# Token-mixing weights in two rings, first copies on two engines, and an order made with the time between successive operations

## The chip, the cores and the metric

The kernel runs on one core of a Trainium2 chip. A core has five engines, each with an instruction stream of its own that it works off in order: TensorE (PE in the profile; PEld is its loading of weights, which overlaps the matmuls), VectorE (DVE), ScalarE (ACT), GpSimd (POOL) and SyncE (SP), which here only issues DMAs. An instruction waits at the head of its stream until what it needs is there, and all that stand behind it wait too. The metric is the device time of one execution in microseconds (us); the median of the runs is what counts.

## The reference: what is computed

```
scores = q @ k.T / sqrt(64);  rel = i - j                      # 4 batches, 8 heads, 576 tokens, 64 wide
scores = where(0 <= rel < 128, scores - slope_h * |rel|, -1e9) # a causal window with a linear bias
x = softmax(scores) @ v                                        # -> (4, 576, 512)
xt = x.transpose(0, 2, 1)
u = x + (relu(xt @ w_tok1) @ w_tok2).transpose(0, 2, 1)        # token mixing, 576 -> 256 -> 576
u = u + relu(u @ w_ch1) @ w_ch2                                # channel layer, 512 -> 1536 -> 512
y = u + relu(layernorm(u) * g @ b_ch1) @ b_ch2                 # channel layer, 512 -> 2048 -> 512
```

## The kernel before

The 2304 tokens are 18 tiles of 128 rows. The attention goes tile by tile. For tile i TensorE makes the scores of its two halves of heads (bank `ps_s`, L625); VectorE merges the two key tiles by a predicated copy (L660) and adds the bias while it takes the row's extreme (L666); ScalarE takes the exponentials and their sums (L675, eight of 128 columns a tile); TensorE transposes them (L682, into `ps_t`, one bank); ScalarE copies the transposed half to `pf` (L384); GpSimd cuts it by the two triangles (L692); TensorE multiplies by `v` (L637, into the one bank `ps_v`, in one piece with the scores of a later tile); ScalarE copies the sum to `ut`, TensorE transposes it back (L704), VectorE divides (L400, `u`).

A finished tile goes into the token mixing. Every such product is made as three matmuls of a rounded part and a remainder (`xh`, `xl`; `wt1h`, `wt1l`): L469 to L471 for the first matrix, L764 to L766 for the second, whose weights lie in `fewh` and `fewl`. ScalarE makes the rounded parts, GpSimd most remainders of weights and tiles, in two halves each. The channel layers follow from about 140 us, by seven products instead of eight (L1125 to L1127) and second products (L1238 to L1240, L1275), each with its own conversions.

The weights lie in DRAM as 64-bit floats, and `load_f64` (L410) converts a piece on the chip: one DMA brings the bytes with the exponents ("heads", tile `rh`), one the bytes with the fractions (`rw`). ScalarE reads `rh` (L445, to `e`), VectorE makes sign and exponent `s` (L448, L450), the fraction `m` (L452) and the value `y` (L460); then ScalarE rounds `y` and GpSimd takes the remainder. There is one buffer `rh` and there are two `rw`, for all weights: the next piece's heads are sent for when ScalarE has read the last. The first token matrix is five pieces of 256 columns, the second four of 288; the ring `w` of six tiles (pool `wa`) stays empty until the channel weights come, from the 12th half tile on.

What stands where on each engine is decided when the program is built. The planner (class `Plan`, L121) takes operations with a cost for each engine that can do them, plays them through engine by engine, and takes at each engine the available one with the earliest due time (`ranks`, L207, `order`, L223). `LAT` (L136) is what it adds between the end of an operation and the start of one that needs it; `dve`, `act`, `pool_tt` and `pe` (L313 to L334) give costs by columns. Remainders and sums may go to VectorE or GpSimd, whichever it finds ready sooner, with 1200 ns to VectorE's disadvantage (`SPARE`). `TOK_RATE` lets three steps of token mixing follow each half tile.

Of the kernel before, what the change touches and what calls it, by code (L numbers as in the profile page):

```python
# [24 lines left out]
P = 128  # L25
# [7 lines left out]
RING = 4  # L33
CT = 4
# [86 lines left out]
class Plan:  # L121
# [14 lines left out]
    LAT = {"PE": 400, "DVE": 260, "ACT": 290, "POOL": 180, "DMA": 4000, "CTL": 0}  # L136
# [192 lines left out]
def pe(n):  # L329
    return 2.6 + n / 2.4  # L330


def pe2(n):
    return 13 + n / 2.4  # L334


def block_kernel(tc, qT, kT, v, wt1, wt2, wa1, wa2, wb1, wb2, g, bias, out):
# [72 lines left out]
    def load_f64(src, k, n, dst=None, get=None):  # L410
# [5 lines left out]
        rh = buf("raw", [P, DM, 4], I16, "rh", 1)  # L416
# [10 lines left out]
        def head(dt):  # L427
            return rh.t[:, :n, 3].bitcast(dt) if dt != I16 else rh.t[:, :n, 3]

        def load_half(x, first):  # L430
            def emit():
                out, in_ = rows(x.t[:, :n].bitcast(U8), first)
                nc.sync.dma_start(out=out, in_=in_)

            op({"DMA": max(P * n * 8 / 360, 500)}, emit, writes=[x])

        load_half(rh, at)
        load_half(rw, at + 3)

        def half(x):  # L440
# [5 lines left out]
            out=e.t[:, :n], in_=head(BF16), func=AF.Copy, scale=2.0 ** -116), [rh], [e])  # L446

        op({"DVE": 1.3 * dve(n // 2, True)}, lambda: nc.vector.tensor_scalar(  # L448
            half(s), half(e), 3, EXP16, ALU.logical_shift_left, ALU.bitwise_and), [e], [s])
        op({"DVE": 1.3 * dve(n // 2)}, lambda: nc.vector.scalar_tensor_tensor(  # L450
            out=half(s), in0=half(e), scalar=SIGN16, in1=half(s), op0=ALU.bitwise_and, op1=ALU.bitwise_or), [e], [s])
        op({"DVE": 1.3 * dve(n, True)}, lambda: nc.vector.tensor_scalar(  # L452
# [7 lines left out]
        op({"DVE": 1.3 * dve(n)}, lambda: nc.vector.scalar_tensor_tensor(  # L460
            out=get(), in0=m.t[:, :n], scalar=2.0 ** 32, in1=s.t[:, :n], op0=ALU.add, op1=ALU.mult), [m, s], [dst])
# [120 lines left out]
    def load_wt2(j):  # L582
        kt, c = divmod(j, 2)
        w = S // 2
# [22 lines left out]
    def packed(i, i2):  # L607
# [21 lines left out]
        if i2 is not None:  # L629
            tiles2 = keys_of(i2)[0]  # L630
            na = len(tiles2)
            for c in range(2):
# [7 lines left out]
                parts.append((na * 440, values, [(pf_t[i2, c], a) for a in range(na)] + [vs[kt] for kt in tiles2],  # L640
# [11 lines left out]
    def softmax(i, c):  # L652
# [5 lines left out]
        if na == 2:  # L658
            b = slice((1 - own) * P, (2 - own) * P)
            op({"DVE": 690}, lambda: nc.vector.copy_predicated(  # L660
# [4 lines left out]
        for m in range(4):  # L665
            op({"DVE": 358}, lambda m=m: nc.vector.tensor_tensor_reduce(  # L666
# [7 lines left out]
        for m in range(4):  # L674
            op({"ACT": 580}, lambda m=m: nc.scalar.activation(  # L675
# [8 lines left out]
        op({"PE": 400}, transposes, [pr, ident], [pt])  # L684

        pf = pf_t[i, c] = buf("atb", [P, 2, 4, P], F32, "pf", PF_BUFS)
        if na == 1:
            copy((pf, 0), lambda: pf.t[:, 0], pt, lambda: pt.t, 4 * P, ("ACT",), True)
        else:
            copy((pf, 1), lambda: pf.t[:, 1], pt, lambda: pt.t, 4 * P, ("ACT",), True)  # L690
            for a in range(2):
                op({"POOL": 630}, lambda a=a: nc.gpsimd.affine_select(  # L692
# [3 lines left out]
    def normalize(i):  # L696
# [3 lines left out]
        copy(ut, lambda: ut.t, pv, lambda: pv.t, DM, ("ACT",), True)  # L700
# [5 lines left out]
        op({"PE": 400}, transposes, [ut, ident], [pv])  # L706
# [44 lines left out]
    def tok2(i):  # L751
        parts = batches_of(i)
        o = buf("pst", [P, DM], F32, "tok", 2)
        for m, (b, r0, n, s0) in enumerate(parts):
# [3 lines left out]
            for kt in range(2):  # L758
                hh, hl = h1_t[b, kt]
                pieces = ["zero"] + sorted({kt * 2 + first // (S // 2), kt * 2 + (end - 1) // (S // 2)})  # L760
# [15 lines left out]
    def attention():  # L776
# [37 lines left out]
        for i in range(-1, NTILE + 1):  # L814
# [15 lines left out]
            for c in range(2):  # L830
# [29 lines left out]
    def turned(layer, places):  # L860
# [6 lines left out]
        if layer == 1:  # L867
            x = buf("mlp", [P, 4, P], F32, "st", ST_BUFS)
            for j, (i, k) in enumerate(places):
                op({"ACT": 330}, lambda i=i, j=j, g=get[j]: nc.scalar.activation(  # L870
# [9 lines left out]
        op({"PE": 430}, emit, [*xs, ident], [b])  # L880
# [367 lines left out]
    def second_fast(s, w2, hid):  # L1248
# [17 lines left out]
        def product(group, x, h, w, start, stop):  # L1266
# [11 lines left out]
            op({"PE": 6 * pe2(HW)}, emit, [hh, hl, wh, wl], [o])  # L1278
# [202 lines left out]
```

## Time and profile before

| | us |
|---|---|
| median of 3 runs (lowest, highest) | 834.79 (834.41, 836.09) |
| profiled execution, whole | 835.71 |
| profiled execution, span of its instructions | 834.0 |
| PE busy | 820.6 (98%) |
| PEld, DVE busy | 691.7 (83%), 658.4 (79%) |
| POOL, ACT busy | 466.4 (56%), 430.8 (52%) |
| TensorE's granted clock | 1.00 in every slice but the last |

The profiled execution is 1.7 us longer than its span, and 0.9 us over the median. Busy times are shares of a span with several stages: attention and token mixing to about 140 us, the channel layers after that. A matmul's end is modelled, so a PE that is shown as busy may still start its next matmul late; the wait of a weight load (PEld) then shows it.

### The profile page before, as it was taken

Reading aid. Unit: us, or ns where it says so; the run is one execution under the profiler, and the core shown is the slowest. Engines: PE = TensorE matmul, PEld = TensorE weight load, DVE = VectorE, ACT = ScalarE, POOL = GpSimd, SP = SyncE. Lnnn points to the kernel's source line nnn. Section 1 sums busy time; section 2 is a strip of 40 time slices with the busy share of each in tenths; the row PEclk is TensorE's granted clock in tenths of the full one; section 3 lists DMA queues with packets and bytes.
Section 4 is the critical chain, followed back from the end, with each engine's and each line's share of the span. In section 5 each row is a group of like instructions: output and inputs, shape, how many; then the busy total and the mean of one; then the engine's idle time right before and its main releaser. Section 6 shows DMA issues by size and latency. Waiting matters only on the chain.

```text
span 834.0 us, 14315 instructions
## 1 busy us (share of the span) xinstructions
PE 820.6 (98%) x4732; PEld 691.7 (83%) x4732; DVE 658.4 (79%) x1372; ACT 430.8 (52%) x1015; POOL 466.4 (56%) x708
## 2 busy tenths in 40 slices
PE   8998999999999999999999999999999999999998
PEld 6777788888888898888888888888889889999996
DVE  5786878978898989978889868989666767777785
ACT  6887777633344535234368333447456634444440
POOL 2685366755454667543338666857533656666650
PEclk9999999999999999999999999999999999999999
DMA  8679657443678799977861544888977663443202
GB/s 301 194 215 275 227 173 224 134 158 111 232 252 283 272 335 334 348 266 266 269 238 55 186 158 137 296 306 299 356 250 243 219 226 136 131 141 122 103 26 101
DMA packets 79898, 179.20 MB, mean 215 GB/s; under 512 B 9040, under 2 KB 9168, under 8 KB 79824
## 3 DMA queue, kind: packets, MB, share of 16 engines
q1 hardware_dynamic: 79344, 176.98, 63.3%
q0 software_dynamic: 480, 1.31, 0.6%
q8 instruction: 37, 0.61, 0.3%
q14 instruction: 37, 0.30, 0.1%
HBM read 138.15 MB, written 38.80 MB: 212 GB/s over the span
## 4 chain that ended last, share of the span: by engine, by line
PE 90%; DVE 3%; DMA 3%; ACT 1%; POOL 1%; issue 1%; SPq 0%; ACTq 0%; DVEq 0%; POOLq 0%
PE tok L1238 11%; PE tok L1240 11%; PE tok L1239 10%; PE b L1125 10%; PE b L1126 10%; PE b L1127 10%; PE tok L1275 5%; PE p L1275 4%; PE ps_v L637 3%; PE ps_s L625 2%; PE p L878 2%; PE b L471 2%; PE b L470 2%; PE b L469 2%; PE tok L766 1%; PE tok L764 1%
## 5 line engine op out<-in xcount | busy, mean ns | idle before, releaser
L1243 DVE TENSOR_TENSOR u<-tok,u 128x512 f32<-128x512 f32 x196 | 133.8, 685 | 47.8 <-PE tok L1240 46.1
L1238 PE MATMUL tok<-w2h,hh 128*128 128x512 f32 x392 | 154.2, 393 | 0.2 <-DVE u L1243 0.2
L1240 PE MATMUL tok<-w2h,hl 128*128 128x512 f32 x392 | 153.0, 390 | 0.2 <-DVE hl L958 0.2
L1239 PE MATMUL tok<-w2l,hh 128*128 128x512 f32 x392 | 152.9, 390 | 0.0
L1125 PE MATMUL b<-xh,w1h 128*128 128x512 f32 x384 | 150.4, 392 | 0.0
L1126 PE MATMUL b<-xl,w1h 128*128 128x512 f32 x384 | 149.8, 390 | 0.0
L1127 PE MATMUL b<-xh,w1l 128*128 128x512 f32 x384 | 149.5, 389 | 0.0
L402 POOL TENSOR_TENSOR w1l<-w,w1h 128x256 fp32r<-128x256 f32 (+1 forms) x110 | 77.4, 725 | 103.5 <-ACT w1h L384 99.0
L956 ACT ACTIVATE hh<-b 128x512 fp32r<-128x512 f32 (+1 forms) x112 | 58.7, 542 | 147.1 <-PE b L1127 104.1
L958 DVE SCALAR_TENSOR_TENSOR hl<-b,hh 128x512 fp32r<-128x512 f32 (+1 forms) x112 | 67.4, 617 | 26.3 <-ACT hh L956 25.7
L1240 PEld LDWEIGHTS tok<-w2h,hl 128*128 128x128 f32 x392 | 73.6, 188 | 16.4 <-DVE hl L958 0.8
L1238 PEld LDWEIGHTS tok<-w2h,hh 128*128 128x128 f32 x392 | 73.7, 188 | 15.5 <-DVE u L1243 1.3
L402 POOL TENSOR_TENSOR w1l<-st,w1h 128x256 fp32r<-128x256 f32 x70 | 55.3, 811 | 55.5 <-ACT w1h L384 49.7
L1239 PEld LDWEIGHTS tok<-w2l,hh 128*128 128x128 f32 x392 | 73.7, 188 | 14.3
L1127 PEld LDWEIGHTS b<-xh,w1l 128*128 128x128 f32 x384 | 72.1, 188 | 15.4
L1125 PEld LDWEIGHTS b<-xh,w1h 128*128 128x128 f32 x384 | 72.3, 188 | 13.9 <-DVE b L400 0.2
L1126 PEld LDWEIGHTS b<-xl,w1h 128*128 128x128 f32 x384 | 72.2, 188 | 13.5
L445 ACT ACTIVATE e<-rh 128x512 bf16<-128x512 bf16 (+2 forms) x65 | 41.5, 639 | 62.1 <-DMA rh<-wb 35.6
L675 ACT ACTIVATE pr<-t,mn 128x128 f32<-128x128 f32 x144 | 55.9, 392 | 13.7 <-DVE mn L666 13.7
L692 POOL TENSOR_SCALAR_AFFINE_SELECT pf<-pf 128x512 f32<-128x512 f32 x64 | 42.5, 663 | 30.1 <-ACT pf L384 27.9
L400 DVE TENSOR_TENSOR b<-b,p 128x512 f32<-128x512 f32 x56 | 38.9, 694 | 19.8 <-PE b L1127 18.7
L402 POOL TENSOR_TENSOR st<-w 128x128 f32<-128x128 f32 x68 | 37.3, 573 | 24.1 <-PE tok L1240 5.5
(188 smaller groups left out, 1909.7 us busy)
## 6 DMA issues: line engine op xcount, KB each, us to landing
w<-d SPq DMA_DIRECT2D x86, 256.0 KB, 4.1
rw<-wb SPq DMA_DIRECT2D x32, 512.0 KB, 5.3
rh<-wb SPq DMA_DIRECT2D x32, 512.0 KB, 5.3
rw<-wa SPq DMA_DIRECT2D x24, 512.0 KB, 4.5
rh<-wa SPq DMA_DIRECT2D x24, 512.0 KB, 4.4
d<-y SPq DMA_DIRECT2D x30, 256.0 KB, 5.0
keys<-kT SPq DMA_DIRECT2D x18, 256.0 KB, 4.3
q<-qT SPq DMA_DIRECT2D x18, 256.0 KB, 4.5
```

Source lines behind the costliest of these rows:

```text
L402: ENGINE[e].tensor_tensor(get()[:, c], ga()[:, c], gb()[:, c], alu)
L675: op({"ACT": 580}, lambda m=m: nc.scalar.activation(out=pr.t[:, m], in_=t.t[:, m], func=AF.Exp, bias=mn.t[:, m:m + 1], scale=-1.0, accum_o ...
L956: op({"ACT": act(n, True)}, lambda: nc.scalar.activation(out=hh.t[:, c], in_=go(), func=AF.Relu), [o], [(hh, key)])
L958: mark[0] = op({"DVE": dve(n)}, lambda: nc.vector.scalar_tensor_tensor(out=hl.t[:, c], in0=go(), scalar=0.0, in1=hh.t[:, c].bitcast(F32), ...
L1125: nc.tensor.matmul(g.t, wh.t[:, w], xh.t, start=start and k == 0, stop=False, skip_group_check=True)
L1126: nc.tensor.matmul(g.t, wh.t[:, w], xl.t, start=False, stop=False, skip_group_check=True)
L1127: nc.tensor.matmul(g.t, wl.t[:, w], xh.t, start=False, stop=stop and k == 1, skip_group_check=True)
L1238: nc.tensor.matmul(o.t, hh.t[:, c:c + P], wh.t, start=j == 0, stop=False)
L1239: nc.tensor.matmul(o.t, hh.t[:, c:c + P], wl.t, start=False, stop=False)
L1240: nc.tensor.matmul(o.t, hl.t[:, c:c + P], wh.t, start=False, stop=j == 1)
L1243: op({"DVE": dve(DM)}, lambda o=o, i=i: nc.vector.tensor_tensor(u[i].t, o.t, u[i].t, ALU.add), [o], [u[i]])
L1275: nc.tensor.matmul(o.t[:, p], x()[:, c], y(), start=start and p == 0 and k == 0, stop=stop and p == 1 and k == 2, skip_group_check=True)
```

## The change

It does four things. (1) `load_f64_split` sends the heads of every second piece of the two token matrices to a tile of the ring `w` instead of `rh`, and reads them there. (2) The second token matrix is loaded in 3 pieces of 192 columns for each half instead of 2 of 288, six in all, and the second token product names those pieces. (3) In the first three tiles (`FIRST_TILES`) the copies `pf` and `ut` may go to VectorE too. (4) The planner's costs are set to other numbers: VectorE's, ScalarE's and GpSimd's fixed part is smaller, a 128x512 matmul costs 10 ns more, the exponential 385 in place of 580, the extreme 211 in place of 358, and the latencies are larger. With them the planner makes another order for the whole program. TensorE's instructions are the same in number and shape (4732 matmuls).

```diff
+WT2_PARTS, FIRST_TILES = 3, 3
-    LAT = {"PE": 400, "DVE": 260, "ACT": 290, "POOL": 180, "DMA": 4000, "CTL": 0}
+    LAT = {"PE": 400, "DVE": 340, "ACT": 400, "POOL": 230, "DMA": 4000, "CTL": 0}
...
 def dve(n, fast=False):
-    return 150 + n / (1.92 if fast else 0.97)
+    return 70 + n / (1.92 if fast else 0.97)
 def act(n, psum=False, pointers=0):
-    return 170 + (0.82 if psum else 0.9) * n + 93 * pointers
+    return 60 + (0.82 if psum else 0.9) * n + 93 * pointers
 def pool_tt(n):
-    return 150 + 2.4 * n
+    return 130 + 2.25 * n
 def pe(n):
-    return 2.6 + n / 2.4
+    return 13 + n / 2.4
...
-    def load_f64(src, k, n, dst=None, get=None):
+    def load_f64(src, k, n, dst=None, get=None, heads=None):
-        rh = buf("raw", [P, DM, 4], I16, "rh", 1)
+        if heads is None:
+            rh = buf("raw", [P, DM, 4], I16, "rh", 1)
+
+            def raw_heads():
+                return rh.t[:, :n]
+        else:
+            rh, raw_heads = heads
...
-        load_half(rh, at)
-        load_half(rw, at + 3)
+        load_half(rh, raw_heads, at)
+        load_half(rw, lambda: rw.t[:, :n], at + 3)
...
+    turn_heads = [0]
+
     def load_f64_split(hi, ghi, lo, glo, src, k, n):
-        split(hi, ghi, lo, glo, *load_f64(src, k, n), n, ("ACT",), ("POOL",))
+        heads = None
+        turn_heads[0] ^= 1
+        if not turn_heads[0]:
+            x = buf("wa", [P, DM], F32, "w", W_BUFS)
+            heads = x, lambda: x.t.bitcast(I16).rearrange("p (n t) -> p n t", t=4)[:, :n]
+        split(hi, ghi, lo, glo, *load_f64(src, k, n, heads=heads), n, ("ACT",), ("POOL",))
...
     def load_wt2(j):
-        kt, c = divmod(j, 2)
-        w = S // 2
+        kt, c = divmod(j, WT2_PARTS)
+        w = S // WT2_PARTS
...
-            op({"DVE": 358}, lambda m=m: nc.vector.tensor_tensor_reduce(
+            op({"DVE": 211}, lambda m=m: nc.vector.tensor_tensor_reduce(
...
-            op({"ACT": 580}, lambda m=m: nc.scalar.activation(
+            op({"ACT": 385}, lambda m=m: nc.scalar.activation(
...
+        on = ("ACT", "DVE") if i < FIRST_TILES else ("ACT",)
         pf = pf_t[i, c] = buf("atb", [P, 2, 4, P], F32, "pf", PF_BUFS)
         if na == 1:
-            copy((pf, 0), lambda: pf.t[:, 0], pt, lambda: pt.t, 4 * P, ("ACT",), True)
+            copy((pf, 0), lambda: pf.t[:, 0], pt, lambda: pt.t, 4 * P, on, True)
...
-        copy(ut, lambda: ut.t, pv, lambda: pv.t, DM, ("ACT",), True)
+        copy(ut, lambda: ut.t, pv, lambda: pv.t, DM, ("ACT", "DVE") if i < FIRST_TILES else ("ACT",), True)
...
-                elif r == 0 and 5 <= m < 9:
+                elif r == 0 and 5 <= m < 5 + 2 * WT2_PARTS:
                     load_wt2(m - 5)
...
-    arrays["wt2"] = rows(w2.reshape(2, P, 2, S // 2).transpose(0, 2, 1, 3), S // 2)
+    arrays["wt2"] = rows(w2.reshape(2, P, WT2_PARTS, S // WT2_PARTS).transpose(0, 2, 1, 3), S // WT2_PARTS)
```

SyncE's stream of DMAs, after the loads of the first tiles; before, where the numbers behind the names only tell buffers apart:

```order
L376 DMA v_189<-v 128x512
L433 DMA rh_199<-wt1 128x2048
L796 DMA bias_sb_131<-bias 128x2048
L561 DMA keys_108<-kT 128x512
L376 DMA q_228<-qT 128x512
L433 DMA rw_238<-wt1 128x2048
L433 DMA rw_245<-wt1 128x2048
```

The same place now:

```order
L373 DMA v_198<-v 128x512
L805 DMA bias_sb_131<-bias 128x2048
L568 DMA keys_108<-kT 128x512
L373 DMA q_226<-qT 128x512
L433 DMA rh_239<-wt1 128x2048
L433 DMA rw_248<-wt1 128x2048
L433 DMA w_253<-wt1 128x2048
L433 DMA rw_261<-wt1 128x2048
L433 DMA w_270<-wt1 128x2048
L433 DMA w_280<-wt2 128x1536
```

The first heads have moved behind the bias table, the keys and the queries of the fifth tile; five more loads of weights follow them at once, three of these into `w`. ScalarE's stream still has the read of the first heads (L445) ahead of the first copy to `ut`, as before.

TensorE's stream after the first values of the second tile; before (`ps_t` is the transpose of exponentials, `ut` the copied sum):

```order
L682 MATMUL ps_t_412<-ident_101,pr_340 128x128 x4
L704 MATMUL ps_v_271<-ident_101,ut_420 128x128 x4
L469 MATMUL tok_444<-xh_395,wt1h0_384 128x512
L470 MATMUL tok_444<-xl_422,wt1h0_384 128x512
L471 MATMUL tok_444<-xh_395,wt1l0_405 128x512
L469 MATMUL tok_452<-xh_395,wt1h0_384 128x512
```

The same place now:

```order
L689 MATMUL ps_t_437<-ident_101,pr_350 128x128 x4
L476 MATMUL tok_447<-xh_370,wt1h0_374 128x512
L477 MATMUL tok_447<-xl_394,wt1h0_374 128x512
L478 MATMUL tok_447<-xh_370,wt1l0_410 128x512
L476 MATMUL tok_459<-xh_370,wt1h0_374 128x512
L477 MATMUL tok_459<-xl_394,wt1h0_374 128x512
L478 MATMUL tok_459<-xh_370,wt1l0_410 128x512
L712 MATMUL ps_v_275<-ident_101,ut_453 128x128 x4
```

The transpose that needs `ut` has gone from ahead of six token matmuls to behind them; from the second to the ninth tile it now has three or six of them in front, where before it had none or three.

VectorE's stream where a tile's scores come in; before:

```order
L709 RECIPROCAL rc_489<-rc_489 128x8
L400 TENSOR_TENSOR u_324<-ps_v_271,rc_400 128x512
L448 TENSOR_SCALAR s_558<-e_479 128x128
L450 SCALAR_TENSOR_TENSOR s_558<-e_479,s_558 128x128
L460 SCALAR_TENSOR_TENSOR y_568<-m_473,s_558 128x256
L452 TENSOR_SCALAR m_577<-rw_362 128x256
L660 COPY_PREDICATED ps_s_585<-after_111,ps_s_585 128x4x128
L660 COPY_PREDICATED ps_s_594<-after_111,ps_s_594 128x4x128
```

The sixth tile now:

```order
L397 TENSOR_TENSOR u_338<-ps_v_275,rc_372 128x512
L717 RECIPROCAL rc_613<-rc_613 128x8
L448 TENSOR_SCALAR s_627<-e_619 128x128
L667 COPY_PREDICATED ps_s_608<-after_111,ps_s_608 128x4x128
L450 SCALAR_TENSOR_TENSOR s_627<-e_619,s_627 128x128
L667 COPY_PREDICATED ps_s_622<-after_111,ps_s_622 128x4x128
```

The step on a piece's heads that needs ScalarE's `e` now stands directly ahead of the tile's predicated copies, or between them, in the fourth to the seventh tile. Over the whole program VectorE has 46 instructions more: 8 for the two added pieces, 2 copies `pf`, and 36 remainders and sums that were on GpSimd, most of 512 columns, nearly all in the channel layers.

## Rows read from the trace of the kernel before

**Rows 1.** Busy time by stretch: PE, PEld, DVE, ACT, POOL; clock, DMA share, GB/s.
```profile
0.00:20.00 20.00, 15.86 (x124) 12.87 (x124) 10.66 (x62) 14.26 (x57) 5.29 (x20) 1.00 0.86 303
20.00:68.00 48.00, 45.38 (x442) 35.34 (x439) 37.69 (x166) 40.59 (x149) 36.42 (x65) 1.00 0.74 208
68.00:76.00 8.00, 5.84 (x59) 4.27 (x58) 4.59 (x23) 4.27 (x15) 2.27 (x6) 1.00 0.92 314
...
100.00:834.00 734.00, 729.53 (x3913) 620.49 (x3912) 587.25 (x1048) 353.16 (x729) 411.45 (x600) 1.00 0.62 211
```

**Rows 2.** Waits of PE in the whole span: us in total, times, longest.
```profile
PE ps_v L704 <- ACT ut L384: 1.5, 3, 0.7
...
PE tok L470 <- POOL xl L402: 0.8, 2, 0.4
PE tok L766 <- POOL fewl L402: 0.6, 1, 0.6
PE tok L1275 <- DVE u L1243: 0.4, 1, 0.4
PE tok L764 <- ACT fewh L384: 0.3, 1, 0.3
PE tok L1238 <- DVE u L1243: 0.2, 1, 0.2
PE tok L1240 <- DVE hl L958: 0.2, 1, 0.2
```

**Rows 3.** Waits of PE's weight loads from 5 to 100 us.
```profile
PEld ps_v L704 <- ACT ut L384: 2.9, 5, 0.9
...
PEld tok L470 <- POOL xl L402: 1.8, 3, 0.7
```

**Rows 4.** ACT in order of time: start, us, instruction, idle time before it and releaser.
```profile
72.45 0.46 ACT L445 ACTIVATE e<-rh 128x288 bf16<-128x288 bf16 x1 [3.73 <-DMA rh<-wt]
72.82 0.58 ACT L384 ACTIVATE pf<-ps_t 128x512 f32<-128x512 f32 x1
```

**Rows 5.** DMA issues from 8.5 to 11.9 us: count, size, us to landing.
```profile
bias_sb<-bias SPq DMA_DIRECT2D x1, 512.0 KB, 6.0
rh<-wt SPq DMA_DIRECT2D x1, 256.0 KB, 5.4
keys<-kT SPq DMA_DIRECT2D x1, 256.0 KB, 5.9
q<-qT SPq DMA_DIRECT2D x1, 256.0 KB, 5.9
```

**Rows 6.** SyncE in order of time: when two of those were issued.
```profile
8.84 0.33 SPq L433 DMA_DIRECT2D rh<-wt  x1
...
10.94 0.33 SPq L376 DMA_DIRECT2D q<-qT  x1
```

**Rows 7.** ACT in order of time, at the first piece's heads.
```profile
14.46 0.43 ACT L445 ACTIVATE e<-rh 128x256 bf16<-128x256 bf16 x1
14.79 0.58 ACT L384 ACTIVATE ut<-ps_v 128x512 f32<-128x512 f32 x1
```

**Rows 8.** PE in order of time: a transpose, the scores of tiles 4 and 9.
```profile
15.43 0.66 PE L704 MATMUL ps_v<-ident,ut 128*128 128x128 f32 x4 [0.16 <-ACT ut L384]
...
18.32 2.00 PE L625 MATMUL ps_s<-keys,q 64*128 64x256 f32 x16
...
55.43 2.00 PE L625 MATMUL ps_s<-keys,q 64*128 64x256 f32 x16
```

**Rows 9.** Groups by line and shape, ACT up to 80 us: busy us, mean ns.
```profile
L675 ACT ACTIVATE pr<-t,mn 128x128 f32<-128x128 f32 x88 | 34.1, 392 | 8.1 <-DVE mn L666 8.1
...
L384 ACT ACTIVATE xh<-u 128x512 fp32r<-128x512 f32 x7 | 4.3, 621 | 0.0
```

**Rows 10.** Groups by line and shape, DVE in the whole span.
```profile
L1243 DVE TENSOR_TENSOR u<-tok,u 128x512 f32<-128x512 f32 x196 | 133.8, 685 | 47.8 <-PE tok L1240 46.1
...
L400 DVE TENSOR_TENSOR w1l<-w,w1h 128x512 fp32r<-128x512 f32 x10 | 7.6, 760 | 1.1 <-ACT w1h L384 0.8
```

More of the change, by code (lines that the diff above doesn't have):

```diff
@@ L425, in rows, with load_half @@
             return x.rearrange("p n t -> p (n t)"), flat[first:first + P * n * 8].rearrange("(p b) -> p b", p=P)
-        def head(dt):
-            return rh.t[:, :n, 3].bitcast(dt) if dt != I16 else rh.t[:, :n, 3]
-        def load_half(x, first):
+        def load_half(x, get, first):
             def emit():
-                out, in_ = rows(x.t[:, :n].bitcast(U8), first)
+                out, in_ = rows(get().bitcast(U8), first)
                 nc.sync.dma_start(out=out, in_=in_)
             op({"DMA": max(P * n * 8 / 360, 500)}, emit, writes=[x])
-        load_half(rh, at)
-        load_half(rw, at + 3)
+        load_half(rh, raw_heads, at)
+        load_half(rw, lambda: rw.t[:, :n], at + 3)
         def half(x):
@@ L638, in values @@
                                                  pf.t[:, a, 2 * p + j], start=(a == 0), stop=(a == na - 1))
-                parts.append((na * 440, values, [(pf_t[i2, c], a) for a in range(na)] + [vs[kt] for kt in tiles2],
+                parts.append((na * 480, values, [(pf_t[i2, c], a) for a in range(na)] + [vs[kt] for kt in tiles2],
                               [(pv, c)]))
@@ L682, in transposes @@
                 nc.tensor.transpose(pt.t[:, m], pr.t[:, m], ident.t)
-        op({"PE": 400}, transposes, [pr, ident], [pt])
+        op({"PE": 436}, transposes, [pr, ident], [pt])
+        on = ("ACT", "DVE") if i < FIRST_TILES else ("ACT",)
         pf = pf_t[i, c] = buf("atb", [P, 2, 4, P], F32, "pf", PF_BUFS)
         if na == 1:
-            copy((pf, 0), lambda: pf.t[:, 0], pt, lambda: pt.t, 4 * P, ("ACT",), True)
+            copy((pf, 0), lambda: pf.t[:, 0], pt, lambda: pt.t, 4 * P, on, True)
         else:
-            copy((pf, 1), lambda: pf.t[:, 1], pt, lambda: pt.t, 4 * P, ("ACT",), True)
+            copy((pf, 1), lambda: pf.t[:, 1], pt, lambda: pt.t, 4 * P, on, True)
             for a in range(2):
-                op({"POOL": 630}, lambda a=a: nc.gpsimd.affine_select(
+                op({"POOL": 606}, lambda a=a: nc.gpsimd.affine_select(
                     pf.t[:, a], pf.t[:, 1], [[0, 4], [1 - 2 * a, P]], (ALU.is_ge, ALU.is_gt)[a], 0.0,
@@ L704, in transposes @@
                 nc.tensor.transpose(pv.t[:, p], ut.t[:, p], ident.t)
-        op({"PE": 400}, transposes, [ut, ident], [pv])
+        op({"PE": 436}, transposes, [ut, ident], [pv])
         rc = buf("small", [P, H, 1], F32, "rc", 2)
@@ L759, in tok2 @@
                 hh, hl = h1_t[b, kt]
-                pieces = ["zero"] + sorted({kt * 2 + first // (S // 2), kt * 2 + (end - 1) // (S // 2)})
+                w = S // WT2_PARTS
+                pieces = ["zero"] + [kt * WT2_PARTS + k for k in range(first // w, (end - 1) // w + 1)]
                 last = m == len(parts) - 1 and kt == 1
@@ L878, in emit @@
                 nc.tensor.transpose(b.t[:, j * P:(j + 1) * P], g(), ident.t)
-        op({"PE": 430}, emit, [*xs, ident], [b])
+        op({"PE": 436}, emit, [*xs, ident], [b])
         return b
@@ L1276, in emit @@
                                          stop=stop and p == 1 and k == 2, skip_group_check=True)
-            op({"PE": 6 * pe2(HW)}, emit, [hh, hl, wh, wl], [o])
+            op({"PE": 6 * pe(HW)}, emit, [hh, hl, wh, wl], [o])
         def fork(group):
```

15 lines of the change are left out of this document (7 added, 8 removed).

## The prediction

> **What bounds the kernel now.** I read the busy time by stretch first. TensorE is the bound almost everywhere: from 100 us on it is busy for 729.53 of 734.00 us [rows 1]. Its instructions are the same in number and shape after the change, so all that can be won or lost is time in which TensorE does not work: 20.00 - 15.86 = 4.14 us in the first 20, 2.62 up to 68, 2.16 from there to 76, and 4.47 after 100 [rows 1]. Of the last 4.47 the waits that have a name are 0.4 + 0.2 + 0.2 = 0.8 us, all for VectorE [rows 2]; the rest lies behind the last matmul. The reader is to see that the attention, a tenth of the span, holds most of the idle time, and that there VectorE, ScalarE and GpSimd are at 37.69, 40.59 and 36.42 of 48 us [rows 1]: none is full, but each runs its stream in order.
>
> Then the waits, by name. TensorE waits 1.5 us in three places for ScalarE's copy `ut`, 0.8 us in two for GpSimd's remainder `xl`, 0.6 and 0.3 us for the second token weights [rows 2]. The weight loads show more for the same causes, 2.9 and 1.8 us [rows 3], since a busy PE can still start late. Last the streams themselves: at 72.45 ScalarE has stood 3.73 us before the heads of a token piece, and behind that read stood the copy `pf` that TensorE needed [rows 4]. This is the 2.16 us between 68 and 76.
>
> **The change part by part.** Durations are those of the profiled execution, 835.71 us long with a span of 834.0; it lies 0.9 us above the median of 834.79, and I carry the difference that I work out over to the median unchanged.
>
> *The last heads.* The late read of heads was late because its DMA could only be sent when `rh` had been read, behind a 512 KB piece of channel weights on SyncE. With three of the six second pieces sent ahead into `w`, the last ones on `rh` follow smaller transfers. I take the 2.16 us as won; the bounds are 0 (the heads are late again) and ScalarE's whole 3.73 [rows 1, 4]. I stay at the row nearest to TensorE. What is late next there is the remainder `fewl` from GpSimd, which the finer pieces bring sooner as well.
>
> *The transpose behind the token matmuls.* Three or six matmuls now stand between the values and the transpose of `ut`, so the copy has time. The waits for `ut` and `xl` are 1.5 + 0.8 = 2.3 us by TensorE's rows and 2.9 + 1.8 = 4.7 by its weight loads' [rows 2, 3]; the middle is 3.5, less 0.16 for the one at 15.43 us, which is counted below [rows 8]: 3.3 won, bounds 2.1 and 4.5.
>
> *The first heads.* This part costs. Before, the first heads are issued at 8.84 and land 5.4 us later, at 14.2; ScalarE reads them at 14.46, at once [rows 5 to 7]. Now the bias table, the keys and the queries go first. These four transfers, the same bytes in another order, ended with the queries at 10.94 + 5.9 = 16.8 us [rows 5, 6]; the heads, now the last of the four, should land then. ScalarE's read still stands ahead of the first copy to `ut` and of the next `pf`, so both move by 16.8 - 14.46 = 2.4 us [rows 7], and with them TensorE's transpose at 15.43 and the scores at 18.32 [rows 8]. Little of it is absorbed: TensorE had 0.16 us idle here before that transpose [rows 8]. I take +2.4. The bounds are 0 (ScalarE comes late to the read) and 3.7, the longest that ScalarE waited for heads [rows 4]. The Trainium skill says, in "DMA: Bandwidth & Descriptors", section Queues, rings and completion order, that completion is not first in, first out per issuing engine; by it the heads could land ahead of what was issued before them, and the sum below would be as low as -4.2. In this trace the four were issued some 0.7 us apart and took 5.4 to 6.0 us each [rows 5, 6], so they landed in the order of issue, and I give that little weight.
>
> *The steps on heads among the predicated copies.* In four tiles VectorE now waits for ScalarE's `e` ahead of a tile's second, or both, predicated copies; behind them stand the extremes, for those wait the exponentials, and for these TensorE's transposes. ScalarE's `e` in turn stands behind the copy `xh` in these tiles. If `xh`, 0.62 us [rows 9], is all that is too much in a tile, four tiles cost 2.5 us; if ScalarE is early, nothing. The lower bound is -0.5, since fuller queues ahead may also take small gaps away; the upper one is taken at the rival below, +3.2. I take +1.3, the middle of 0 and 2.5.
>
> *The copies on VectorE, the two added pieces.* Two copies `pf` go from ScalarE to VectorE, in the first and the third tile. A 128x512 read from a bank takes VectorE 0.69 us [rows 10], much like ScalarE's 0.58 [rows 4]; the first moves nothing, the third stands behind the first piece's steps and is late with them, which is in the term of the first heads. The added pieces are two `e`, two rounded parts, eight VectorE and four GpSimd instructions, beside TensorE's 45.38 us of work up to 68 [rows 1]: 0, and if ScalarE lacked the room two `xh`-like instructions of 0.62 us each, 1.2.
>
> *The order from 100 us on.* VectorE takes 36 operations from GpSimd, at 0.76 us each [rows 10] 27 us in 734, and goes from 587 to about 615 us busy, 84% [rows 1]. That is hidden by TensorE's 729.53 as long as no product waits for its remainder. I take 0: at best the 0.8 us of today's waits for VectorE go [rows 2], at worst I allow three times that again, +2.4. A rule speaks against this part: the Trainium skill, "SBUF — State Buffer", section Who interferes with whom, says that a VectorE instruction with two SBUF inputs contends with a GpSimd instruction that reads SBUF, and that the second to start is blocked whole. The rows agree in kind: `w1l` from two SBUF tiles takes 760 ns where the sum with a bank takes 685 [rows 10], though 75 ns is far from a whole instruction. By the row the 36 cost 2.7 us of VectorE's time, by the rule about 28 us, and then I would put the upper end of this term into the sum.
>
> The sum: -2.2 - 3.3 + 2.4 + 1.3 + 0 + 0 = -1.8 us. The profiled execution would go from 835.7 to 833.9, and the median from 834.8 to 833.0.
>
> **The rivals.** *The first wait is absorbed.* If ScalarE reaches the first heads late, because its exponentials wait for the copy that VectorE now makes among the extremes, and if `e` comes in time, only the gains are left: -2.2 - 3.3 + 0.5 for what is lost at the start, -5.0 in all, 829.8. For it: ScalarE was at 40.59 of 48 us and its costs in the planner now are near the trace's (385 for an exponential that takes 392, 580 before) [rows 1, 9]. Against it: the read at 14.46 came with no wait before it, two instructions after its inputs [rows 7].
>
> *The late heads stay.* The second ring does not do what it says where the DMA itself is the limit. The engines are at 0.86 of their time in the first 20 us and at 0.92 from 68 to 76 [rows 1], and the second matrix's last heads and the first channel weights' still share `rh`; ScalarE would stand before one of those reads, with `pf` behind it. The 2.16 us are then not won: -1.8 + 2.2 = +0.4, 835.2.
>
> *The loop between ScalarE and VectorE sets the tile's period.* This one ends slower. From the end of one tile's `e` VectorE does two steps of the piece and two predicated copies of about 0.7 us each (the sum of a bank's 128x512, [rows 10]) before the first exponential can start, about 2.2 us; then ScalarE has eight exponentials of 0.39, three copies of about 0.55, `xh` and the next rounded part and `e`, about 5.6 [rows 4, 7, 9], and the loop closes: 7.8 us. Before, a tile takes (55.43 - 18.32) / 5 = 7.42 us [rows 8]. It decides wherever the loop is longer than that: +0.35 us a tile over the nine tiles in which pieces are converted, +3.2, and the gain of the moved transpose is not had, since TensorE then waits for exponentials anyway. With the first heads and the late ones this makes 3.2 + 2.4 - 2.2 = +3.4, 838.2. Against it: only four tiles have the steps ahead of a predicated copy, and ScalarE can do exponentials of the other half meanwhile.
>
> **How the numbers follow.** Measurements of this kernel can tell about 0.2%, 1.7 us, from no change. I give the forecast 0.50, and it lies near that edge: 0.26 of it is faster, 0.20 the same and 0.04 slower. The absorbed wait gets 0.20, all faster; the late heads 0.13, all the same; the loop 0.17, all slower. So faster 0.46, the same 0.33, slower 0.21. For the range: the forecast's own terms give 829.4 when two of them lie at their low ends together (the first heads at 0, the transpose at 4.5: -1.8 - 2.4 - 1.2), and 837.1 at their high ends (the last heads at 0, the predicated copies at 3.2: -1.8 + 2.2 + 1.9). The absorbed wait lies at the lower edge, with half of it below, and most of the loop lies above. 829.6 to 837.0 leaves out about a tenth on each side.
>
> **What would show it.** In the changed kernel's profile: ScalarE's first read of heads at 16.8 us with about 2.4 us idle before it, released by a DMA, and the fourth tile's scores near 20.8 in place of 18.32; no wait of ScalarE for heads near 72 us; PE's waits for `ut` and `xl` gone from the list, except one near the start; the ninth tile's scores at 56 to 58; after 100 us the same idle time within 1 us, VectorE near 84%. I am wrong if the first read does not wait, if ScalarE stands again before a DMA between 55 and 75 us, if waits of PE for exponentials (`pr`) take the place of those for `ut`, or if waits for VectorE after 100 us grow beyond 2 us.

## The result and the profile after

The changed kernel takes 845.25 us (844.39 to 845.98), the kernel before on the same chip 834.60 (833.96 to 836.09): 1.0114 times as long, 95% interval 1.0096 to 1.0132. The forecast was 833.0, the range 829.6 to 837.0. The profiled execution took 844.39 us with a span of 842.7. I read it in the order of the prediction. Busy time by stretch, columns as in [rows 1]:

```profile
0.00:20.00 20.00, 14.29 (x104) 11.64 (x104) 10.68 (x61) 11.43 (x47) 3.71 (x17) 1.00 0.90 325
20.00:68.00 48.00, 44.41 (x411) 34.65 (x412) 39.60 (x164) 39.81 (x151) 37.95 (x71) 1.00 0.75 216
68.00:76.00 8.00, 8.00 (x80) 6.51 (x78) 7.11 (x28) 6.82 (x24) 5.41 (x10) 1.00 0.99 360
...
100.00:842.70 742.70, 732.03 (x3936) 619.09 (x3932) 605.09 (x1092) 351.57 (x732) 362.36 (x524) 1.00 0.61 207
```

TensorE loses more in the first 68 us, nothing from 68 to 76, and after 100 us it is idle for 10.67 us instead of 4.47. Its busy time there is not comparable, since less of its work was done by 100 us. To set two executions side by side without the windows' edges I use two marks: the first matmul of the channel layers, and the last matmul of their second matrix. Before, then after:

```profile
159.02 0.39 PE L1125 MATMUL b<-xh,hh 128*128 128x512 f32 x1
...
829.90 0.39 PE L1240 MATMUL tok<-w2h,hl 128*128 128x512 f32 x1
```

```profile
158.57 0.48 PE L1134 MATMUL b<-xh,hh 128*128 128x512 f32 x1
...
838.30 0.39 PE L1249 MATMUL tok<-w2h,hl 128*128 128x512 f32 x1
```

Up to the first mark the change gains 0.45 us; between the marks the channel layers take 679.73 us instead of 670.88, 8.85 more. The whole loss is there, in the part that I put at 0. (The two profiled executions differ by 8.7 us, the medians by 10.65. The changed kernel's profiled execution was the fastest of its four; what the others lost beyond it is in no trace.) Busy time from mark to mark, before and after:

```profile
159.02:830.29 671.27, 670.51 (x3443) 571.84 (x3441) 536.43 (x907) 311.27 (x608) 372.31 (x543) 1.00 0.63 212
158.57:838.69 680.12, 673.46 (x3445) 571.14 (x3443) 558.83 (x944) 311.12 (x608) 329.19 (x472) 1.00 0.62 210
```

TensorE is idle for 6.66 us instead of 0.76, and the same work is counted as busy for 2.95 us more. I read this last third of the loss as matmuls that start late and are shown as busy, since the weight loads wait longer for `u` and `hl` than the matmuls do. From 100 to 830 us, before and after:

```profile
PEld tok L1238 <- DVE u L1243: 1.3, 3, 0.7
...
PEld tok L1240 <- DVE hl L958: 0.8, 2, 0.6
```

```profile
PEld tok L1247 <- DVE u L1252: 4.9, 7, 1.6
PEld tok L1249 <- DVE hl L967: 2.9, 2, 1.5
```

The waits by name, PE in the whole span, which answer to [rows 2]:

```profile
PE ps_t L689 <- ACT pf L381: 3.0, 2, 1.7
PE ps_v L712 <- ACT ut L381: 2.9, 4, 2.0
PE tok L1247 <- DVE u L1252: 2.4, 5, 1.2
PE tok L1249 <- DVE hl L967: 2.1, 2, 1.1
...
PE b L1134 <- ACT b L381: 1.1, 1, 1.1
PE ps_t L689 <- DVE pf L387: 1.0, 1, 1.0
```

The sum into `u` and the remainder `hl` of the hidden tile, 0.4 + 0.2 + 0.2 us before, now hold TensorE for 4.5 us. VectorE is not alone: of the 6.6 us of waits with a name after 100 us, 1.8 are for ScalarE, before none. The idle time lies in a few stretches where VectorE is nearly full. Four of them after, then the first two before:

```profile
280.00:300.00 20.00, 18.53 (x108) 15.97 (x107) 19.96 (x35) 10.23 (x20) 12.95 (x16) 1.00 0.89 307
...
320.00:340.00 20.00, 18.67 (x88) 14.65 (x88) 20.00 (x39) 8.14 (x16) 17.70 (x28) 1.00 0.87 300
...
450.00:470.00 20.00, 19.32 (x85) 15.02 (x84) 19.20 (x38) 9.42 (x19) 13.94 (x21) 1.00 0.47 171
...
570.00:590.00 20.00, 17.75 (x77) 14.02 (x76) 17.86 (x30) 15.07 (x33) 15.14 (x21) 1.00 0.74 266
```

```profile
280.00:300.00 20.00, 20.00 (x119) 17.70 (x119) 18.56 (x35) 10.28 (x21) 14.22 (x17) 1.00 0.98 340
...
320.00:340.00 20.00, 20.00 (x89) 16.29 (x88) 19.65 (x35) 8.29 (x16) 17.11 (x26) 1.00 0.95 332
```

What happens inside one of them: VectorE after, in order of time (start, us, instruction).

```profile
284.27 0.68 DVE L460 SCALAR_TENSOR_TENSOR y<-m,s 128x512 f32<-128x512 uint32 x1
284.99 0.43 DVE L452 TENSOR_SCALAR m<-rw 128x512 uint32<-128x512 uint32 x1
285.33 1.13 DVE L448 TENSOR_SCALAR s<-e 128x256 int32<-128x256 int32 x1
286.38 1.23 DVE L397 TENSOR_TENSOR w1l<-w,w1h 128x512 fp32r<-128x512 f32 x1
287.53 0.96 DVE L450 SCALAR_TENSOR_TENSOR s<-e,s 128x256 int32<-128x256 int32 x1
288.42 1.27 DVE L967 SCALAR_TENSOR_TENSOR hl<-b,hh 128x512 fp32r<-128x512 f32 x2
```

Five steps of weight conversion, for which TensorE does not wait here, run without a gap; `hl` comes behind them, and TensorE stands there for 1.00 us. The same kind of stall returns at 580.42 and 584.89:

```profile
289.75 0.50 PE L1249 MATMUL tok<-w2h,hl 128*128 128x512 f32 x1 [1.00 <-DVE hl L967]
...
580.42 0.50 PE L1249 MATMUL tok<-w2h,hl 128*128 128x512 f32 x1 [1.06 <-DVE hl L967]
584.89 0.50 PE L1247 MATMUL tok<-w2h,hh 128*128 128x512 f32 x1 [1.19 <-DVE u L1252]
```

### The profile page after: what moved, and what is told of

The parts are those of the page before. It is cut to its first block, busy times and chain, and to the rows that moved or that the text cites. A ratio compares the mean times of both kernels' runs of the same rounds, so it can differ in the third digit from the quotient of the medians.

```text
span 842.7 us, 14273 instructions
## 1 busy us (share of the span) xinstructions
PE 822.7 (98%) x4732; PEld 691.3 (82%) x4732; DVE 682.6 (81%) x1418; ACT 429.0 (51%) x1017; POOL 421.2 (50%) x639
## 4 chain that ended last, share of the span: by engine, by line
PE 61%; DVE 6%; POOL 4%; ACT 2%; issue 2%; DMA 1%; SPq 0%; POOLq 0%; DVEq 0%; ACTq 0%
PE b L1134 8%; PE b L1135 8%; PE tok L1247 8%; PE b L1136 8%; PE tok L1248 8%; PE tok L1249 8%; PE tok L1284 5%; PE p L1284 4%; POOL fewh L399 2%; DVE st L397 2%; PE b L476 1%; PE b L478 1%; PE b L477 1%; DVE u L1252 1%; POOL w1l L399 1%
## 5 line engine op out<-in xcount | busy, mean ns | idle before, releaser
L399 POOL TENSOR_TENSOR w1l<-w,w1h 128x256 fp32r<-128x256 f32 (+1 forms) x100 | 72.4, 746 | 119.9 <-ACT w1h L381 114.1
L445 ACT ACTIVATE e<-rh 128x512 bf16<-128x512 bf16 (+2 forms) x62 | 39.8, 641 | 78.8 <-DMA rh<-wb 46.7
L399 POOL TENSOR_TENSOR w1l<-st,w1h 128x256 fp32r<-128x256 f32 x44 | 36.7, 854 | 64.4 <-ACT w1h L381 53.8
L381 ACT ACTIVATE w1h<-w 128x256 fp32r<-128x256 f32 (+1 forms) x83 | 46.0, 555 | 6.7 <-issue 4.1
```

What stands on the lines that cost most here:

```text
L399: ENGINE[e].tensor_tensor(get()[:, c], ga()[:, c], gb()[:, c], alu)
```

## The experiments

All were timed in five rounds beside the kernel before on the same chip. "First mark" and "channel" come from one profiled execution of each, as above; changes are against before's 159.02 and 670.88 us.

| kernel | median us | ratio to before (95%) | first mark | channel |
|---|---|---|---|---|
| costs_only | 846.36 | 1.0127 (1.0110 to 1.0143) | +0.21 | +9.68 |
| loads_only | 833.90 | 0.9985 (0.9973 to 0.9997) | -1.83 | -0.53 |
| after_old_engines | 841.74 | 1.0071 (1.0054 to 1.0088) | +0.16 | +5.34 |
| before_new_engines | 837.34 | 1.0019 (1.0006 to 1.0032) | +3.13 | +0.77 |
| vec_only | 844.35 | 1.0102 (1.0085 to 1.0120) | +1.66 | +6.56 |
| pe_only | 838.89 | 1.0039 (1.0024 to 1.0053) | -0.83 | +3.55 |
| rest_only | 839.67 | 1.0046 (1.0029 to 1.0064) | +0.61 | +3.11 |
| vec_old | 839.79 | 1.0048 (1.0031 to 1.0066) | -2.38 | +5.83 |
| vec_dear | 846.59 | 1.0130 (1.0110 to 1.0151) | +2.32 | +7.79 |
| urgent | 844.90 | 1.0101 (1.0081 to 1.0121) | +1.64 | +6.77 |
| nudge_vec | 836.03 | 1.0004 (0.9989 to 1.0019) | +2.31 | +1.15 |
| nudge_lat | 836.60 | 1.0009 (0.9994 to 1.0025) | -1.07 | +0.14 |
| vec110 | 836.30 | 1.0003 (0.9992 to 1.0015) | -1.24 | +2.07 |
| vec190 | 839.35 | 1.0053 (1.0038 to 1.0067) | +0.55 | +2.73 |
| rings_pieces | 835.31 | 0.9998 (0.9989 to 1.0008) | -0.31 | -0.55 |
| copies_only | 835.04 | 0.9986 (0.9974 to 0.9998) | -1.71 | -0.55 |
| copies_6 | 835.25 | 0.9987 (0.9973 to 1.0001) | +1.14 | -0.85 |
| copies_18 | 833.37 | 0.9975 (0.9960 to 0.9989) | -1.66 | -1.44 |

Single first marks can be 2 to 3 us off where TensorE's clock fell in that execution (last section). From 160 us on the clock was granted at 1.00 in all of these traces, so the column of the channel layers is free of that. It still stands on one execution each; the medians decide.

**Costs or loads.** The change has two halves: the planner's numbers, and the rings, pieces and first copies. Each ran alone. The edit of `costs_only` is `LAT` and the cost lines of the change on the kernel before; `loads_only` puts the old ones back into the changed kernel, beginning with

```diff
-    LAT = {"PE": 400, "DVE": 340, "ACT": 400, "POOL": 230, "DMA": 4000, "CTL": 0}
+    LAT = {"PE": 400, "DVE": 260, "ACT": 290, "POOL": 180, "DMA": 4000, "CTL": 0}
```

> The kernel before with the new costs and latencies alone (no second ring, two pieces, first copies on ScalarE). Theory A (the new costs change VectorE's work and order in the channel layers, and that is the loss): 6 to 9 us slower than before, 841 to 844 us, with TensorE's idle time after 100 us at about 10 us instead of 4.5. Rival B (the rings, pieces and first copies in the attention part are the loss, and the late steps of the channel layers only pass it on): within 2 us of before.

> The changed kernel with the old costs and latencies: two rings, three pieces and first copies on two engines remain. Theory A: within 2 us of before, 833 to 836 us, and as good as before after 100 us. Rival B: 6 us or more slower than before. My sum for these parts alone was between -5.5 and +1.3 us; 0 would say that the late heads' gain and the first heads' loss cancel.

Theory A holds and B falls: the costs alone lose 11 us, more than the 6 to 9 that A forecast (TensorE is idle for 10.98 us after 100 us, where A said about 10), and the loads alone gain 1.5. `loads_only` has these waits of PE from 100 to 830 us, as few as before:

```profile
PE tok L1288 <- DVE u L1256: 0.4, 1, 0.4
PE b L1138 <- DVE b L401: 0.3, 1, 0.3
```

**Load or order.** The new costs do two things: another choice of engine for 124 of 365 remainders and sums, and another order. Forcing the choice separates them; `ENGINES` holds one letter for each such operation, as the planner chose in the other kernel:

```diff
         rank = self.ranks()
+        free_ops = [k for k, op in enumerate(ops) if len(op[0]) > 1 and "POOL" in op[0]]
...
+        for k, x in zip(free_ops, ENGINES):
+            e = {"D": "DVE", "P": "POOL"}[x]
+            ops[k] = ({e: ops[k][0][e]}, *ops[k][1:])
```

> The changed kernel, its new costs kept for the order, but each remainder and sum that either VectorE or GpSimd may do is put on the engine that does it in the kernel before (80 go back to GpSimd, 44 to VectorE, net 36 off VectorE). Theory A1 (VectorE's load is the loss): most of the 10.6 us comes back, 835 to 838 us, and VectorE's busy time after 100 us falls by about 27 us. Theory A2 (the order by the new due times is the loss, on whichever engine): 843 us or more.

> The kernel before, its costs and loads kept, but each remainder and sum that either VectorE or GpSimd may do is put on the engine that does it in the changed kernel (net 36 more on VectorE). Theory A1 (load): 4 to 9 us slower than before, 839 to 844 us. Theory A2 (order): within 2 us of before.

Neither expectation of load holds. VectorE's 36 more operations, put into the old order, cost the channel layers 0.77 us; taking them out of the new order leaves 5.34 of 8.85. The load is thus worth 3.51 us in the new order and 0.77 in the old one; the order alone is the larger part. The median of `after_old_engines`, 841.74, lies between the two forecasts, that of `before_new_engines` within the 2 us of A2. From 100 to 830 us VectorE is busy for 599.89 us in `before_new_engines` and for 600.24 in the changed kernel, but not in the same places:

```profile
280.00:300.00 20.00, 20.00 (x114) 17.57 (x113) 17.45 (x33) 11.51 (x23) 9.57 (x12) 1.00 0.94 338
320.00:340.00 20.00, 20.00 (x101) 16.96 (x101) 19.16 (x34) 8.95 (x17) 15.68 (x26) 1.00 0.99 334
```

TensorE has no gap: VectorE does 2.5 and 0.8 us less in these stretches than in the changed kernel, and more elsewhere. The median lies 1.9 us over before's, and in the profiled execution most of the difference lies ahead of the first mark. There the clock was granted at 0.91 from 60 to 100 us; the four executions at a mean clock of 1.000 took 835.13 to 836.57 us, so part of the 1.9 is the clock.

**Which numbers.** Theory C starts from a sum that I had not made. With the planner's own costs, added up over its list, what it puts on VectorE after its 100 us is 625 us of work before and 541 us after; measured, it is 587.25 [rows 1] and 605.09. The new numbers let the planner believe in free time that isn't there.

```diff
 def dve(n, fast=False):
-    return 150 + n / (1.92 if fast else 0.97)
+    return 70 + n / (1.92 if fast else 0.97)
```

This with 1.2 for 1.3 in the conversions, 600 for 690 and 211 for 358, alone on the kernel before, is `vec_only`; undone alone in the changed kernel, it is `vec_old`. `pe_only` has TensorE's new numbers alone, `rest_only` the latencies and ScalarE's and GpSimd's; their first lines are

```diff
 def pe(n):
-    return 2.6 + n / 2.4
+    return 13 + n / 2.4
```

```diff
 def act(n, psum=False, pointers=0):
-    return 170 + (0.82 if psum else 0.9) * n + 93 * pointers
+    return 60 + (0.82 if psum else 0.9) * n + 93 * pointers
```

> The kernel before with VectorE's new costs alone. Theory C: 5 to 10 us slower than before, 840 to 845 us, the loss at 280 to 345, 450 to 465 and 570 to 590 us. Rival D: within 2 us of before. If the loss needs both VectorE's cheap costs and TensorE's dearer ones, 1 to 4 us slower.

> The changed kernel with VectorE's old costs alone (150 ns for every operation instead of 70, 1.3 instead of 1.2 in the conversions, 690 and 358 in the attention); everything else new. Theory C (VectorE's new costs are less than its operations take beside GpSimd, so the planner puts work that can wait ahead of work that cannot): most of the loss after 100 us goes, 834 to 838 us. Rival D (the other new numbers, TensorE's above all, reorder the layers): 842 us or more.

> The kernel before with TensorE's new costs alone (13 ns for every matmul instead of 2.6, 436 instead of 400 for four transposes). Theory C: within 2 us of before, 833 to 837 us. Rival D: 5 us or more slower.

> The kernel before with the new latencies and the new costs of ScalarE and GpSimd; VectorE and TensorE keep the old. Theory C: within 2 us of before, 833 to 837 us, since its VectorE gets 126 of the remainders and sums, as many as before (122). Rival D: 4 us or more slower.

VectorE's numbers are the largest single part, 6.56 us in the channel layers and 7.8 by the median, as theory C forecast, with the same kind of wait, `hl` above all:

```profile
PE tok L1240 <- DVE hl L958: 2.9, 3, 1.7
PE b L1127 <- DVE w1l L400: 1.4, 1, 1.4
PE b L1125 <- DVE b L400: 1.0, 1, 1.0
```

But theory C's other half fails: TensorE's numbers and the rest each lose over 3 us there alone (2.3 and 3.1 by the medians, more than C allows and less than D asks), and undoing VectorE's leaves 5.83, with a median between the forecasts of C and D. The three parts alone add up to 13.2, together they cost 9.68 (`costs_only`), so they are not separate terms.

**Is any other number a loss?** Two tiny changes on the kernel before, 155 for 150 in `dve` and 5 ns more in three latencies; then 110 and 190; and 230 in the changed kernel, with VectorE's other numbers as before.

```diff
-    return 150 + n / (1.92 if fast else 0.97)
+    return 155 + n / (1.92 if fast else 0.97)    # nudge_vec; vec110: 110; vec190: 190; vec_dear: 230
```

```diff
-    LAT = {"PE": 400, "DVE": 260, "ACT": 290, "POOL": 180, "DMA": 4000, "CTL": 0}
+    LAT = {"PE": 400, "DVE": 265, "ACT": 295, "POOL": 185, "DMA": 4000, "CTL": 0}
```

> The kernel before with one number changed a little: 155 ns instead of 150 for every VectorE operation in the planner. Theory E (the order before is one good draw, and any other set of numbers, however near, loses 3 to 4 us after 100 us): 838 to 840 us. Theory C (only numbers that are far from what the engines do lose): within 1.5 us of before.

> The kernel before with three numbers changed a little: the latencies of VectorE, ScalarE and GpSimd 5 ns longer in the planner. Theory E: 838 to 840 us. Theory C: within 1.5 us of before.

> The kernel before with 110 ns instead of 150 for every VectorE operation in the planner, half of the way to the new 70; nothing else. Theory C (too cheap a VectorE is the loss): 2 to 4 us slower than before. Theory V (a loss on either side of 150): the same here.

> The kernel before with 190 ns instead of 150 for every VectorE operation in the planner; nothing else. Theory C: within 1.5 us of before, since a VectorE that is planned too slow makes nothing late. Theory V: 2 to 4 us slower, with TensorE waiting for GpSimd or ScalarE as well as for VectorE.

> The changed kernel with VectorE's costs above the old ones (230 ns for every operation instead of 70, 1.3 in the conversions, 690 and 358 in the attention), so that the planner's sum for VectorE is 775 us where the changed kernel's is 605. Theory C: no slower than with the old costs (839.8 us), and perhaps better, 835 to 840 us, with at most 100 of the 365 remainders and sums on VectorE. Theory E: 838 to 842 us, without a trend.

Theory E falls: the nudges change the medians by nothing that can be told. The middle steps lose on both sides, 2.07 and 2.73 us in the channel layers. At 110 most of this is paid back before the first mark, so its median is before's, where C and V had both forecast 2 to 4 us more. At 230 ns the changed kernel loses more than at the old 150 (7.79 against 5.83). A dearer VectorE has fewer operations, 100 of the 365 against 129, and is no better. So theory V is nearer than C: distance on either side costs, and "too cheap" is not the whole cause. Nor does V hold in full: at 190 PE's waits after 100 us are for VectorE alone, not for GpSimd or ScalarE, and 155 already costs 1.15 us in the channel layers of its trace, so the loss does not simply grow with the distance.

**Would priority mend it?** In `urgent` the two operations that TensorE waited for are ranked 4 us earlier, costs unchanged:

```diff
+        for k in self.urgent:
+            late[k] -= 4000
...
+        pl.urgent.add(mark[0])
...
```

> The changed kernel with the rank of the two VectorE operations that TensorE waited for (the remainder hl of the hidden tile and the sum into u) set 4 us earlier in the planner's list; the costs stay. Theory F (these two stand behind work that could wait, since the planner ranks them late): 3 us or more of the loss come back, 842 us or less. Rival G (in the planner's time they are already first when they are ready; it is the whole VectorE stream that runs late against its plan, by 605 against 541 us after 100 us): within 1.5 us of the changed kernel, 843.5 to 846.5 us.

F falls, and by its median G holds: 844.90 us. In the trace the channel layers get back 2.1 of 8.85 us, more than G allows, while the first mark came 2.1 us later than in the changed kernel (the clock was granted at 0.86 from 20 to 40 us). So rank matters a little at most; that the rest of the late `hl` and `u` are late with VectorE's whole stream is what G says, and no run shows it separately.

**Which load gains.** Second-ring tiles hold 256 columns, so rings need pieces of 192; they ran together, without first copies (`FIRST_TILES = 0`), and the copies ran without them, then in more tiles:

```diff
+WT2_PARTS, FIRST_TILES = 2, 3    # copies_only; copies_6: 2, 6; copies_18: 2, 18; rings_pieces: 3, 0
...
+        on = ("ACT", "DVE") if i < FIRST_TILES else ("ACT",)
```

> The kernel before with two rings of heads and three pieces (the second ring's tiles hold 256 columns, so the one needs the other), without first copies on two engines and with the old costs and latencies. My sum's late heads: 2.2 us faster, less what is lost to heads that share six tiles with the later weights. If the first copies are what made the loads faster: within 0.7 us of before.

> The kernel before with the first copies of three tiles on either ScalarE or VectorE; one ring, two pieces, old costs and latencies. My sum's value for the copy ut alone: up to 3.3 us faster, if the stall before the transposes of the first tiles goes. If the rings carry the gain: within 0.7 us of before.

> The kernel before with the copies pf and ut of the first six tiles, not three, on either ScalarE or VectorE; one ring, two pieces, the old costs. If ScalarE's stream is what TensorE waits for in the attention: 1 us or more faster than with three tiles (835.0), 833 to 834 us. If the first three tiles' copies gave all there is: 834.5 to 836 us.

> The same with all 18 tiles. If ScalarE's stream is the limit: 832 to 834 us. If VectorE, which has 37.7 of 48 us of work from 20 to 68 us, is then late with its extremes: 836 us or more.

The copies carry most of it: alone they have the ratio of both together, and rings and pieces alone change nothing that can be told. In `copies_only` the planner puts four copies on VectorE, two `pf` and two `ut`. What falls most is TensorE's wait for the copies: 1.5 us for `ut` before [rows 2] and 2.6 for `pf` in the same view; with copies in three tiles

```profile
PE ps_t L692 <- ACT pf L385: 1.2, 2, 0.7
...
PE ps_v L715 <- ACT ut L385: 0.7, 1, 0.7
```

and with all tiles, where 22 copies go to VectorE, 0.7 for `pf`, 1.0 for `ut`. New waits take part of it back, 0.9 us for exponentials with three tiles, 1.1 for exponentials and 1.3 for VectorE's step `s` with all. With all tiles ScalarE is relieved of 2.7 us from 20 to 68 us, and VectorE takes 5.4 more [rows 1]:

```profile
20.00:68.00 48.00, 45.35 (x446) 36.32 (x446) 43.13 (x178) 37.88 (x148) 37.04 (x67) 1.00 0.74 216
```

Three, six and 18 tiles give medians of 0.9986, 0.9987 and 0.9975; the intervals overlap, so whether more tiles give more is not settled. `copies_18`, with one ring, two pieces and the old costs, beats both kernels: 833.37 us, 2.6 us below before on the same chip.

## Why the prediction was wrong

*The order from 100 us on* is the step that failed: "I take 0 ... at worst I allow three times that again, +2.4". It cost 8.85, and the range held none of it. I counted the 36 operations that change engine, 27 us against TensorE's 729.53, and asked whether the total fits. The moved work was even less than that, 599.89 - 586.56 = 13.3 us of VectorE's time from 100 to 830 us in `before_new_engines`, and nearly harmless (0.77 us). What I left out is that new costs reorder every engine's stream, and that an in-order stream is late by its order even at 81% busy. Even my slowest rival with the upper end of this term, 838.2 + 2.4, falls short of 845.25. One of my signs did say it: waits for VectorE after 100 us beyond 2 us would show me wrong, and they are 4.5 for `u` and `hl`.

*The first heads*, +2.4, came as worked out: read at 16.91 instead of 14.46 (forecast 16.8), ScalarE idle for 1.79 us (forecast about 2.4), the transpose at 17.88 instead of 15.43, the fourth tile's scores at 20.96 (forecast 20.8) [rows 7, 8]:

```profile
16.91 0.43 ACT L445 ACTIVATE e<-rh 128x256 bf16<-128x256 bf16 x1 [1.79 <-DMA rh<-wt]
17.25 0.58 ACT L381 ACTIVATE ut<-ps_v 128x512 f32<-128x512 f32 x1
```

```profile
17.88 0.66 PE L712 MATMUL ps_v<-ident,ut 128*128 128x128 f32 x4 [1.97 <-ACT ut L381]
...
20.96 2.00 PE L632 MATMUL ps_s<-keys,q 64*128 64x256 f32 x16
...
59.35 0.49 PE L632 MATMUL ps_s<-keys,q 64*128 64x256 f32 x2
```

The heads, issued at 11.02 us, landed 5.9 us later, behind the three transfers issued before them, as I had it. Alone, the costs put this read at 15.02 us and the loads at 15.65; it takes both for 16.91.

*The last heads*, -2.2: the wait went as forecast, the gain is not shown. PE is busy for 8.00 of the 8 us where it had 5.84 [rows 1], and no read of a token piece's heads waits near 72 us, where ScalarE had stood 3.73 us (with rings and pieces alone it stands 0.9); it now waits there for the heads of channel weights, 0.35 us at 69.34 and 0.83 at 75.39. But `copies_18`, with one ring, has 8.00 us in the same stretch too, since stalls move, so the stretch does not measure the ring. The rings and pieces alone brought 0.31 us by the first mark and nothing that can be told in the median.

*The transpose behind the token matmuls*, -3.3, was mis-sized. Without the first one, 1.97 us, the waits for `ut` are 0.9 us against 1.5 less 0.16; by the weight loads they went from 2.9 to 2.6, and for `xl` from 1.8 to 1.3 [rows 3]:

```profile
PEld ps_v L712 <- ACT ut L381: 4.8, 5, 2.2
...
PEld ps_t L689 <- ACT pr L682: 2.3, 6, 1.2
...
PEld tok L477 <- POOL xl L399: 1.3, 4, 0.8
```

That is some 0.8 won of 3.3. The sign that I had named, waits for exponentials (`pr`) in their place, did not come: PE's list has none, and the weight loads waited 2.3 us for them before as well, though never so long at once:

```profile
PEld ps_t L682 <- ACT pr L675: 2.3, 10, 0.3
```

What took the gain is thus not shown.

*The steps among the predicated copies*, +1.3: the waits of PE for `pf` rose from 2.6 us to 3.0 + 1.0, one of them, of 1.35, behind the first heads. The predicted 1.3 has this size, but the two causes were not separated, and the wait that the term goes through, ScalarE's for the extremes (`mn`), hardly rose: 3.9 us from 20 to 68 us, 3.7 before. The ninth tile's scores at 59.35 instead of 55.43 lie beyond my 56 to 58. The sum of the attention's terms was -1.8 and the first mark moved by -0.45. The transpose fell short by 2.5, more than this difference of 1.35; what came back elsewhere was not traced.

*The copies on VectorE*, at 0, may have been wrong in the other direction: in `copies_only` they gain 1.71 us by the first mark. There, though, two copies `ut` move as well as two `pf`, in another order; what the two `pf` of the changed kernel gain was not measured. A copy that takes 0.69 us on one engine and 0.58 on the other is no gain by its length; I take it to be one by the place that it frees in ScalarE's stream.

Of the rivals none was it. The loop between ScalarE and VectorE is not what cost the time, and the side on which I had put most weight, faster, was wrong.

What stays open is why the old numbers give the better order. Their sum for VectorE after 100 us is 6% over what the trace shows, the new ones' 11% under it, but 110 and 190 lie on either side of 150 and both lose in the channel layers, so nearness to the trace alone is not the reason.

## What to carry to other kernels

When a change alters the costs by which a planner orders everything, bound it by the streams: look in the trace for stretches where an engine is nearly full, see what urgent work stands behind work that can wait, and widen the range by what a few such stretches can lose (here 0.7 to 2.3 us of TensorE's time in each of four); the total of moved work says little. Compare the planner's sum for each engine with the busy time that the trace shows. A change that bundles new numbers with other edits should be taken apart first: here a gain of 1.5 us was hidden under a loss of 11.

## What had not been expected of the hardware

TensorE's clock fell after short idle times, and that cost as much as the edits of the loads. `after_old_engines` issues the same first instructions on TensorE as the changed kernel, but its first heads came 0.6 us later, TensorE waited 2.92 us instead of 1.97 for `ut`, and then the clock was granted at 0.50, the lower of its two levels, 1.2 GHz of 2.4:

```profile
15.00:20.00 5.00, 1.69 (x12) 1.15 (x12) 3.88 (x23) 2.50 (x10) 1.03 (x3) 0.97 1.06 393
20.00:25.00 5.00, 4.04 (x18) 3.19 (x20) 3.15 (x7) 3.59 (x15) 3.87 (x8) 0.50 0.77 280
```

```profile
18.46 0.66 PE L724 MATMUL ps_v<-ident,ut 128*128 128x128 f32 x4 [2.92 <-ACT ut L393]
...
22.00 3.79 PE L644 MATMUL ps_s<-keys,q 64*128 64x256 f32 x16
```

The same scores took 2.00 us at full clock. The length of one stall does not decide it alone: in the profiled execution of `copies_6` TensorE had waited 0.69 us at 11.27 and 0.88 at 12.80, and the clock was granted at 0.50 from 14 to 16 us:

```profile
12.80 0.63 PE L692 MATMUL ps_t<-ident,pr 128*128 128x128 f32 x4 [0.88 <-ACT pr L685]
13.36 3.68 PE L635 MATMUL ps_s<-keys,q 64*128 64x256 f32 x16
```

Executions of one kernel part mostly by this: the five of `copies_6` with a mean clock of 0.996 to 0.998 took 835.51 to 837.04 us, the four fastest, at 1.000, took 832.93 to 833.30; three others, at 0.999 and 1.000, took 833.33 to 835.50. A stall early in the kernel can thus cost twice.

VectorE's instructions were lengthened beside GpSimd's more than the 75 ns of [rows 10]: the step `s` at 285.33 took 1.13 us where it took 0.28 at 584.76, and the remainder `w1l` at 286.38, which reads two SBUF tiles, 1.23 us beside a GpSimd product, where it took 0.67 at 290.88 with GpSimd idle. The Trainium skill, "SBUF — State Buffer", section Who interferes with whom, says that a VectorE instruction with two SBUF inputs contends with a GpSimd instruction that reads SBUF, and for this single instruction the trace agrees. The sum that I worked out from it does not come out: the 36 operations added 13.3 us to VectorE in `before_new_engines`, 0.37 us each, where I worked out 28 us of contention by that rule. That figure is net. GpSimd is 51.6 us less busy there (359.89 after 411.45 from 100 to 830 us), and some of VectorE's other instructions are shorter: `y` from 128x512 inputs took 787 ns on the mean against 851 before. I take the one to be the cause of the other; no run separates them.
